# Weights of eight channel steps at staggered start addresses in an attention, gating and mixing kernel

## The chip, the core and the metric

The kernel runs on one core of one Trainium2 chip. The metric is the device time of a run in microseconds, the median of three runs. TensorE does the matmuls: it loads 128 columns of weights (the stationary operand) and then streams the moving operand past them, 512 columns at most. VectorE, ScalarE and GpSimd do the element-wise work, and SyncE, GpSimd and ScalarE issue DMAs. The on-chip memory SBUF has 128 partitions; a tile takes the same range of byte addresses in each of them, and all start addresses below are byte addresses within a partition.

## The reference

```python
scores = scale * q @ k^T - log(S)            # 4 batches, 12 heads, S = 448, head 64
x  = sigmoid(scores) @ v                     # -> x of 4 x 448 x 768
g  = sigmoid(causal_conv5(x, conv_w))
x  = (g * (x @ w_val)) @ w_out
u  = x + (relu(x^T @ w_tok1) @ w_tok2)^T     # token mixing
out = u + relu(u @ w_ch1) @ w_ch2            # channel mixing, 768 -> 1536 -> 768
```

The weights come as 64-bit floats, whose words the kernel decodes itself into a high and a low part of 32 bits. A product of two such split numbers takes three matmuls (high by high, low by high, high by low).

## The kernel before

The kernel runs through three stages. The first is attention, two heads at a time (lines 256 and 271). The second goes batch by batch through the value and output projections (line 334, 448 columns), the transposes (line 357) and the two token products (lines 374 and 387). The third is the channel stage, which is what the change touches.

The channel stage works on the 1792 rows of u in four column tiles of 512, 512, 384 and 384 (`TILES`). For each of them it goes through 12 channel steps of 128 hidden channels. `ch1(t, fc)` multiplies u by the step's part of `w_ch1` (18 matmuls: 6 row blocks of 768, three each; line 674); ScalarE and VectorE make the relu and its split into a high and a low tile `r` (lines 86 and 88). `ch2(t, fc)` multiplies `r` by the step's part of `w_ch2` into six accumulators (18 matmuls, line 695). The order is written by hand: ch1 of the next step stands ahead of ch2 of the step before, so that blocks of 18 matmuls of ch1 and ch2 alternate and the relu of one step lies beside a block of the other. Between two blocks nothing else runs on TensorE.

The weights of a step are four tiles side by side of 768 columns of 4 bytes: the high and the low part for ch1, and the same for ch2. They stay in SBUF for all four column tiles. Steps 1 to 3 lie in tiles `w` on the left side of SBUF, which the value projection used before; step 0 lies in a tile `wch0` on the left, and steps 4 to 11 each in a tile `wch4` to `wch11` of 12,288 bytes on the right side, where they are allocated one after the other from step 11 to step 4 (`wch_alloc`, at the start of the channel stage). In the kernel before, the right-hand tiles lie at 122,624 (wch11), 134,912 (wch10) and so on in steps of 12,288 up to 208,640 (wch4), all of them multiples of 256. So do all other tiles that TensorE reads in this stage: the moving operands (`us`, the split u, and `r`) and the tiles `w` and `wch0`. Two small tiles, `pad_l` of 160 bytes and `pad_r` of 224 bytes, stand at the outer ends of both sides.

The tile of step 4 is filled by four DMAs from a scratch area in HBM (`pre_load`, line 613, on GpSimd's queue), since its weights were decoded earlier. Steps 5 to 11 are decoded during the first column tile: two loads on SyncE's queue for each step (lines 578 and 583), and then for each a chain of operations that ends with a product on VectorE (line 132, the low part) and a copy on ScalarE (line 140, the high part) into the wch tile. They are given a low priority, so that the evictions of the matmuls go ahead of them.

Of the kernel before, what the change touches and what calls it, by code (L numbers as in the profile page):

```python
# [10 lines left out]
F32R = mybir.dt.float32r  # L11
# [19 lines left out]
def tile_kernel(ctx, tc, qT, kT, v, w_val, conv_w, w_out, w_tok1, w_tok2, w_ch1, w_ch2, out):  # L31
# [10 lines left out]
    DM = H * D  # L42
    P = 128
# [527 lines left out]
    wch, us_t, acc, r_t = {}, {}, {}, {}  # L571
    wch_t, r_b = {}, []
# [40 lines left out]
                nc.gpsimd.dma_start(wch[fc][which][a], wscr[PRE.index(fc), which, a])  # L613

    def wch_alloc(pool, fc):
        wch_t[fc] = pool.tile([P, 2, 2, DM], F32R, name=f"wch{fc}")

    def dec_ch(fc):
        for which in range(2):
# [85 lines left out]
    with tc.manual_schedule():  # L705
# [23 lines left out]
        for b in range(B):  # L729
            val, outs, t1, t2 = dense_steps(b)  # L730
            if b:

                weave(val[0] + back1 + sum(val[1:], []) + back2, first.pop(0), 0.95)
            else:
                val = sum(val, [])
                for n in (12, 8, 4):
                    val.insert(n, (0, dec_step))
                weave(val, [])
                assert not (begun or raws or decs)
                dec.release()  # L740
                dn["late"] = tc.alloc_tile_pool(name="late", bufs=1, side="right", reuse_waits="tile")
                pre = tc.alloc_tile_pool(name="pre", bufs=1, side="left")
                ops = ch_ops(pre, [(fc, which) for fc in PRE for which in range(2)])
                first = [ops[: len(ops) // 2], ops[len(ops) // 2 :]]
            if b + 1 < B:
                weave(outs, post_ops(b + 1))
            else:
                os = outs + t1 + t2
            back1, back2 = t1, t2
            if b + 2 == B:  # L750
                pre.release()
                xbp.release()
                rp["a"] = tc.alloc_tile_pool(name="p2a", bufs=1, side="left")
                wch_alloc(rp["a"], 0)
                first.append(ch_ops(rp["a"], [(0, 0), (0, 1)]))
# [15 lines left out]
    for fc in range(KF - 1, CHAN_HELD - 1, -1):  # L771
        wch_alloc(rp["p"], fc)
# [63 lines left out]
```

## Time and profile before

| | us |
|---|---|
| three runs | 731.84, 732.78, 732.80 |
| median | 732.78 |
| span of the profiled execution | 729.8 |
| TensorE matmuls busy | 724.2 (99%) |
| TensorE weight loads busy, beside the matmuls | 594.1 (81%) |
| VectorE busy | 398.9 (55%) |
| ScalarE busy | 256.7 (35%) |
| GpSimd busy | 40.2 (6%) |

The span runs from the first to the last instruction of one profiled execution. It has no timed run of its own; the difference to the median, 3.0 us, is what lies around it. The page calls TensorE's matmuls PE and its weight loads PEld. Matmuls are pipelined: one lasts 389 ns at 512 columns, but the next begins before it ends, so the pace is read from the starts of blocks and not from the length of one.

### The profile page before, as it was taken

How to read it: one execution, taken by the hardware profiler on the slowest of the kernel's cores; microseconds unless marked ns; L12 is line 12 of the kernel's file. 1: busy time of each engine (PE TensorE's matmuls, PEld its weight loads, DVE VectorE, ACT ScalarE, POOL GpSimd, SP SyncE). 2: the span in 40 equal slices, each digit the busy share in tenths (PEclk: the TensorE clock that was granted, in tenths of full speed). 3: DMA queues.
4: the chain of work that ended last, by engine and by line, in shares of the span. 5: the costliest groups of instructions: out<-in, count | busy, mean ns of one | idle time of the engine just before them, and what ended most of it. 6: DMA issues, size and time to landing. Idle time of an engine off the chain costs nothing.

```text
span 729.8 us, 10824 instructions
## 1 busy us (share of the span) xinstructions
PE 724.2 (99%) x4360; PEld 594.1 (81%) x4360; DVE 398.9 (55%) x690; ACT 256.7 (35%) x379; POOL 40.2 (6%) x90
## 2 busy tenths in 40 slices
PE   8999999999999999999999999999999999999998
PEld 3344444799999999999998888888888899999997
DVE  1899766489889878965577999320100400040002
ACT  6899888344334333422343434200000200020000
POOL 0001100000111111002012000000000000000000
PEclk9999999999999999999999999999999999999999
DMA  9847997221344232044927453250000610042001
GB/s 298 252 153 236 266 299 234 83 91 47 102 150 147 76 127 101 17 147 131 311 82 227 162 172 127 67 172 0 1 0 1 201 38 0 1 128 67 1 1 65
DMA packets 56737, 87.24 MB, mean 120 GB/s; under 512 B 8032, under 2 KB 48240, under 8 KB 56688
## 3 DMA queue, kind: packets, MB, share of 16 engines
q1 hardware_dynamic: 50352, 62.86, 28.1%
q0 software_dynamic: 5904, 23.23, 9.0%
q8 instruction: 34, 0.56, 0.3%
q10 hardware_dynamic: 432, 0.46, 0.2%
q14 instruction: 15, 0.12, 0.1%
HBM read 66.68 MB, written 19.86 MB: 119 GB/s over the span
## 4 chain that ended last, share of the span: by engine, by line
PE 98%; ACT 1%; DVE 1%; issue 0%; ACTq 0%
PE psd L334 24%; PE psh L674 24%; PE pso L695 24%; PE pss L256 8%; PE psy L271 8%; PE pst L374 4%; PE pst L387 4%; PE pst L357 1%; ACT ga L258 1%; PE psi L718 0%; DVE dec_a L123 0%; DVE w L132 0%; ACT dec_a L111 0%; DVE dec_e L129 0%; DVE ur L701 0%
## 5 line engine op out<-in xcount | busy, mean ns | idle before, releaser
L88 DVE SCALAR_TENSOR_TENSOR r<-psh,r 128x384 fp32r<-128x384 f32 (+1 forms) x47 | 29.3, 623 | 213.4 <-ACT r L86 213.4
L674 PE MATMUL psh<-us,wch 128*128 128x512 f32 (+1 forms) x648 | 135.5, 362 | 0.0
L695 PE MATMUL pso<-r,wch 128*128 128x384 f32 (+1 forms) x630 | 131.1, 361 | 0.0
L674 PEld LDWEIGHTS psh<-us,wch 128*128 128x128 f32 x648 | 117.3, 188 | 12.7
L695 PEld LDWEIGHTS pso<-r,wch 128*128 128x128 f32 x630 | 113.8, 188 | 11.9
L86 ACT ACTIVATE r<-psh 128x384 fp32r<-128x384 f32 (+1 forms) x47 | 25.5, 543 | 230.7 <-PE psh L674 230.6
L334 PE MATMUL psd<-gv,wo 128*128 128x448 f32 x432 | 92.3, 369 | 0.0
L258 ACT ACTIVATE ga<-pss,bias_s 128x896 f32<-128x896 f32 x84 | 83.6, 1005 | 19.0 <-PE pss L256 18.2
L334 PE MATMUL psd<-xs,w 128*128 128x448 f32 x432 | 89.9, 367 | 0.0
L334 PEld LDWEIGHTS psd<-xs,w 128*128 128x128 f32 x432 | 80.9, 188 | 8.2 <-issue 0.7
L334 PEld LDWEIGHTS psd<-gv,wo 128*128 128x128 f32 x432 | 80.2, 188 | 6.6
L256 PE MATMUL pss<-q,k 64*64 64x448 f32 x672 | 78.5, 537 | 1.0 <-ACT ga L258 0.9
L271 PE MATMUL psy<-ga,v 64*64 64x448 f32 x672 | 77.6, 536 | 0.0
L304 DVE SCALAR_TENSOR_TENSOR gate<-xb,cw,gate 128x448 f32<-128x448 f32 x96 | 65.7, 685 | 2.8
L256 PEld LDWEIGHTS pss<-q,k 64*64 64x64 f32 x672 | 26.0, 133 | 39.4 <-issue 29.0
L271 PEld LDWEIGHTS psy<-ga,v 64*64 64x64 f32 x672 | 25.7, 133 | 37.4 <-issue 35.9
L111 ACT ACTIVATE dec_a<-dec_a,exp_b 128x768 int32<-128x768 int32 (+3 forms) x43 | 36.8, 868 | 37.1 <-DVE dec_a L108 37.1
L123 DVE SCALAR_TENSOR_TENSOR dec_a<-raw,dec_a 128x768 int32<-128x768 int32 (+2 forms) x42 | 37.3, 888 | 19.7 <-ACT dec_a L111 19.7
L674 PE MATMUL psh<-us,w 128*128 128x512 f32 (+1 forms) x216 | 45.2, 362 | 0.0
L695 PE MATMUL pso<-r,w 128*128 128x512 f32 (+1 forms) x216 | 45.1, 362 | 0.0
L674 PEld LDWEIGHTS psh<-us,w 128*128 128x128 f32 x216 | 39.1, 188 | 4.3
L695 PEld LDWEIGHTS pso<-r,w 128*128 128x128 f32 x216 | 39.1, 188 | 4.2
(80 smaller groups left out, 648.7 us busy)
## 6 DMA issues: line engine op xcount, KB each, us to landing
raw<-w_ch SPq DMA_DIRECT2D x24, 768.0 KB, 4.4
v<-v SPq DMA_DIRECT2D x24, 224.0 KB, 6.5
uscr<-x2T POOLq DMA_DIRECT2D x24, 224.0 KB, 3.7
q<-qT SPq DMA_DIRECT2D x23, 224.0 KB, 4.3
k<-kT SPq DMA_DIRECT2D x22, 224.0 KB, 4.5
raw<-w_out POOLq DMA_DIRECT2D x6, 768.0 KB, 8.4
wscr<-pre POOLq DMA_DIRECT2D x12, 384.0 KB, 3.6
xscr<-xb SPq DMA_DIRECT2D x18, 224.0 KB, 4.7
```

What stands on the lines that cost most here:

```text
L88: nc.vector.scalar_tensor_tensor(out=l_out, in0=src, scalar=0.0, in1=f(h_out), op0=ALU.max, op1=ALU.subtract)
L111: nc.scalar.activation(out=t["a"], in_=t["a"], func=AF.Relu, scale=8.0, bias=exp_b)
L123: nc.vector.scalar_tensor_tensor(out=t["a"], in0=hi, scalar=-0x80000000, in1=t["a"], op0=ALU.bitwise_and, op1=ALU.bitwise_or)
L256: nc.tensor.matmul(ps[cols, j, :S], k[rows, keys], q[rows], start=True, stop=True)
L258: nc.scalar.activation(out=a, in_=ps[:, :, :S], func=AF.Sigmoid, bias=bias_s, scale=QK_SCALE)
L271: nc.tensor.matmul(y_t[i + h][cols, :S], v_t[i][rows, c, cols], a[rows, j], start=c == 0, stop=c == NB - 1)
L304: nc.vector.scalar_tensor_tensor(out=acc, in0=x[:, t : t + S], scalar=w, in1=acc, op0=ALU.mult, op1=ALU.add)
L334: nc.tensor.matmul(ps[:, :S], w(a, kk), s[:, c, :], start=kk == 0 and n == 0, stop=kk == KD - 1 and n == 2,)
L374: nc.tensor.matmul(ps[:, :HALF], a, x[:, m], start=n == 0, stop=n == len(mm) - 1)
L387: nc.tensor.matmul(ps[:, :S], a, m[:, t, :], start=t == 0 and n == 0, stop=t == KT - 1 and n == 2)
L674: nc.tensor.matmul(ps[:, :n_t], wch[fc][0][a][:, kk * P : (kk + 1) * P], us_t[t, kk][:, c, :], start=kk == 0 and n == 0, stop=kk == KD - 1 ...
L695: nc.tensor.matmul(acc[j][:, :n_t], wch[fc][1][a][:, j * P : (j + 1) * P], r[c], start=fc == 0 and n == 0, stop=fc == KF - 1 and n == 2,)
```

## The change

The tile of a step is allocated with 8 more elements of 4 bytes at its end, for all steps but step 0, and its first 4 x 768 columns are used as before. Since the eight tiles of steps 11 to 4 lie one after the other down from the same upper end, each begins 32 bytes further off a multiple of 256 than the next higher step: wch11 at 122,368 (0 modulo 256), wch10 at 134,688 (32), wch9 at 147,008 (64), wch8 at 159,328 (96), wch7 at 171,648 (128), wch6 at 183,968 (160), wch5 at 196,288 (192) and wch4 at 208,608 (224). No other tile moves. Each engine has the same instructions in the same order with the same waits as before.

```diff
     def wch_alloc(pool, fc):
-        wch_t[fc] = pool.tile([P, 2, 2, DM], F32R, name=f"wch{fc}")
+        t = pool.tile([P, 4 * DM + (8 if fc else 0)], F32R, name=f"wch{fc}")
+        wch_t[fc] = t[:, : 4 * DM].rearrange("p (n a m) -> p n a m", n=2, a=2)
```

## Rows read from the trace of the kernel before

**Rows 1.** The page: span; TensorE's busy time, share, instructions; its granted clock, 40 slices.
```profile
span 729.8 us, 10824 instructions
...
PE 724.2 (99%) x4360; PEld 594.1 (81%) x4360; DVE 398.9 (55%) x690; ACT 256.7 (35%) x379; POOL 40.2 (6%) x90
...
PEclk9999999999999999999999999999999999999999
```

**Rows 2.** The page: the chain that ended last, share of the span by line.
```profile
PE psd L334 24%; PE psh L674 24%; PE pso L695 24%; PE pss L256 8%; PE psy L271 8%; PE pst L374 4%; PE pst L387 4%; PE pst L357 1%; ACT ga L258 1%; PE psi L718 0%; DVE dec_a L123 0%; DVE w L132 0%; ACT dec_a L111 0%; DVE dec_e L129 0%; DVE ur L701 0%
```

**Rows 3.** Waits of TensorE in the whole run: us in total, times, longest.
```profile
PE psi L718 <- DVE zero L707: 1.2, 1, 1.2
PE pss L256 <- ACT ga L258: 0.9, 3, 0.4
```

**Rows 4.** Timeline of TensorE: start us, length us, line, output and inputs, columns, count.
```profile
409.04 4.24 PE L674 MATMUL psh<-us,wch 128*128 128x512 f32 x18
413.12 4.24 PE L695 MATMUL pso<-r,w 128*128 128x512 f32 x18
417.19 4.24 PE L674 MATMUL psh<-us,wch 128*128 128x512 f32 x18
...
466.15 4.01 PE L674 MATMUL psh<-us,wch 128*128 128x512 f32 x17
```

**Rows 5.** The chain in order of time: start us, us, what.
```profile
568.32 4.08 PE pso L695 x18
572.40 3.14 PE psh L674 x18
575.54 4.12 PE pso L695 x18
579.66 3.14 PE psh L674 x18
...
604.65 3.12 PE psh L674 x18
```

**Rows 6.** Matmuls in four short stretches from 575.4 us: busy us, mean ns of one.
```profile
L695 PE MATMUL pso<-r,wch 128*128 128x512 f32 x10 | 2.5, 393 | 0.0
...
L695 PE MATMUL pso<-r,wch 128*128 128x512 f32 x9 | 2.2, 389 | 0.0
...
L674 PE MATMUL psh<-us,w 128*128 128x384 f32 x7 | 1.4, 338 | 0.0
...
L674 PE MATMUL psh<-us,w 128*128 128x384 f32 x12 | 2.2, 334 | 0.0
```

**Rows 7.** Timeline of TensorE, projections of 448 columns, in two stretches.
```profile
132.73 22.15 PE L334 MATMUL psd<-xs,w 128*128 128x448 f32 x108
154.72 1.58 PE L334 MATMUL psd<-gv,wo 128*128 128x448 f32 x7
...
194.42 18.75 PE L334 MATMUL psd<-xs,w 128*128 128x448 f32 x90
213.01 0.57 PE L387 MATMUL pst<-wt2H,h 128*128 128x448 f32 x2
```

**Rows 8.** Weight loads by form: busy us, mean ns of one, idle before.
```profile
L674 PEld LDWEIGHTS psh<-us,wch 128*128 128x128 f32 x648 | 117.3, 188 | 12.7
...
L357 PEld LDWEIGHTS pst<-ident,x2T 128*128 128x128 f32 x96 | 11.9, 140 | 1.7
```

**Rows 9.** Two stretches: us, busy us and count of each engine, granted clock, DMA.
```profile
409.00:474.20 65.20, 65.20 (x289) 53.98 (x288) 51.38 (x74) 25.72 (x34) 0.00 (x0) 1.00 0.40 127
...
598.00:648.00 50.00, 50.00 (x291) 50.00 (x290) 7.49 (x14) 6.97 (x14) 0.00 (x0) 1.00 0.04 10
```

**Rows 10.** Timelines: VectorE's last product into a wch tile; GpSimd's four DMAs for wch4.
```profile
455.29 0.96 DVE L132 SCALAR_TENSOR_TENSOR wch<-raw,dec_e 128x768 fp32r<-128x768 f32 x1
...
386.18 2.18 POOL L613 DMA_DIRECT2D wch<-wscr  x4
```

**Rows 11.** DMA issues: KB each, median us from issue to landing.
```profile
wch<-wscr POOLq DMA_DIRECT2D x4, 384.0 KB, 6.5
```

## The prediction

> **What bounds the kernel now.** I read the page first: the span is 729.8 us, TensorE is busy for 99% of it, and its granted clock is at full in all 40 slices [rows 1]. The span is the profiled execution's own; the three timed runs have a median of 732.78 us, so about 3.0 us of a run lie outside the span, and I add these 3.0 us to every span below. The shares of the chain that ended last come next: nearly all of it is TensorE, and the two lines of the channel stage, 674 and 695, hold 24% each [rows 2]. The waits of TensorE add up to 2.1 us in the whole run, all of it near the start [rows 3]. So no transfer, no decode and no eviction is late anywhere in the channel stage, and what decides the time there is the pace at which one matmul follows another.
>
> The pace is read from the blocks of 18 matmuls that ch1 and ch2 issue in turn. A block on the weights w, a block on the weights wch and the next one start 4.07 to 4.08 us apart [rows 4], and the chain gives 4.08 us for a block of 512 columns and 3.12 us for one of 384 [rows 5]. That is 226.7 and 173.3 ns for a matmul. The 128 columns between them cost 53.3 ns, so 512 columns by themselves are 213.3 ns, and every matmul pays 13.3 ns on top, at either width.
>
> **What the change does, part by part.** The order of instructions and the waits are the same on every engine before and after; what differs is where eight tiles begin. wch11 stays at a multiple of 256 bytes, wch10 begins 32 bytes past one, wch9 64, and so on to wch4 at 224. All other operands of TensorE in this stage (us, r, w, wch0) keep starting at multiples of 256. Three things touch the moved tiles.
>
> First, what fills them: 14 products of the decode on VectorE and 14 copies on ScalarE write wch5 to wch11, and four DMAs fill wch4. The last VectorE product starts at 455.29 us and takes 0.96 us [rows 10]; the first block that reads wch11 starts at 466.15 us [rows 4], so there are 9.9 us of room. In the stretch from 409 to 474 us VectorE is busy for 51.4 of 65.2 us [rows 9]; even if each of the 14 products took twice its 0.96 us, the 13.4 us more would still fit in the 13.8 us that are free. The DMAs for wch4 are issued by 388.4 us [rows 10], land some 6.5 us later [rows 11], and the first block on wch4 starts at 409.04 us [rows 4]: 14 us of room. I cost all this at nothing, hidden by TensorE's own blocks; the cover would be gone only if a write became some ten microseconds late.
>
> Second, the size: each tile is 32 bytes longer, the eight together reach 256 bytes lower, and no wait was added by that. Nothing.
>
> Third, TensorE's weight loads, which is all that is left. Seven of the eight steps (4 to 10) have a new offset. A step has 36 matmuls on each of four column tiles, so 7 x 36 x 4 = 1008 weight loads and matmuls, 504 at 512 columns and 504 at 384, in 56 blocks of 18. The trace of before has no matmul of this kind with a weight that begins off a multiple of 256 bytes, so the cost has to be bounded by the nearest rows.
>
> That the pace isn't fixed by the instruction alone does stand in the trace. Where the width switches, the block takes longer for a while: the 512-column block that follows one of 384 columns took 4.12 us where the others take 4.08, and the two 384-column blocks beside it 3.14 where the others take 3.12 [rows 5]. Inside them it is the first matmuls: the first ten of the 512-column block last 393 ns each, the later nine 389; at 384 columns 338 for the first seven and 334 for the later ones [rows 6]. So a stream that is disturbed runs about 4 ns a matmul slower until it falls back into its regular beat. The 448-column projections show the same without any switch: 108 matmuls from 132.73 to 154.72 us are 203.6 ns each, 90 matmuls of the same form from 194.42 to 213.01 us are 206.6 ns each [rows 7], where halfway between the paces at 384 and 512 columns would be 200.0. The same form on the same tiles thus has more than one beat, 3.0 ns apart.
>
> The weights' offset changes at the border of blocks: into ch1 of step 4 (0 to 224), out of it into ch2 of step 3 (224 to 0), then at every border until the block after ch2 of step 10, 17 borders on each column tile, 68 in all, half at each width. **Low end of the forecast:** each such border disturbs the beat as a switch of width does, 34 x 0.04 + 34 x 0.02 = 2.0 us. **High end:** the 1008 matmuls never find a good beat. With the 4 ns of a disturbed stream that is 4.0 us; with the 6.6 ns by which the slow beat at 448 columns stands over 200.0 it is 6.6 us. I take the low end, 2.0 us, since a change of operand at the border of a block is nearest to the rows of the switch, where the beat was found again within the block; the other ends go into the range.
>
> Below nothing: no row shows a matmul of the channel stage at a lasting faster beat, but the 13.3 ns that each pays on top of its columns are there to be lost, 1008 x 13.3 = 13.4 us at the very most. The only gain of which a row gives the size is the 3.0 ns between the two beats at 448 columns, 1008 x 3.0 = 3.0 us.
>
> The sum: 729.8 + 2.0 = 731.8 us of span, and with the 3.0 us around it **734.8 us**.
>
> **The rivals.** *No difference.* The offset of the weights may not matter to TensorE at all. For it speaks that w, wch0 and wch stand at different multiples of 256 bytes and that ch1 takes its moving operand from us and ch2 from r, and yet their blocks are alike to 0.01 us [rows 4, 5]: none of these address bits shows. Against it speaks that these rows hold only multiples of 256, and that the beat reacts to small disturbances. The time is then that of before, 732.8 us. The Trainium skill has a rule for this (TensorE: Matmul & The Clock Gate, Step-by-step: what each phase is for): TensorE reads the moving operand and the weights through two independent ports of SBUF, so that loading the next weights takes nothing from the running matmul. By that rule nothing of the change can reach the pace, and the time stays. The trace bears it out only in part: load and matmul do overlap, but the 13.3 ns on top and the two beats at 448 columns are not explained by columns alone.
>
> *Faster.* If the 13.3 ns come from weight and moving reads that meet because both begin at multiples of 256, a spread of starts would thin them out. With the 3.0 ns above this is 729.8 us in a run. It decides if most of the seven offsets have a better beat than 0. Against it: the disturbances in rows 5 and 6 all go up, and the regular beat is the best that these blocks show.
>
> *The weight load becomes the bound.* At 384 columns the weight loads leave no gap, 50.00 of 50.00 us [rows 9], and one takes 188 ns [rows 8] where a matmul follows each 173.3 ns. How long a load is does vary between forms: the one of the transposes, 128 columns of 4 bytes as well, takes 140 ns [rows 8]. If a start off 256 bytes made a load touch three stretches of 256 bytes instead of two, I bound what that could add by this difference of 48 ns: 504 x 48 = 24.2 us at 384 columns; at 512 columns 226.7 - 188 = 38.7 ns hide the first part and 504 x 9.3 = 4.7 us remain. Together 28.9 us, 761.7 us. It decides from the point where a load is visibly longer than 188 ns. Against it: the length of a load did not react in any block, at either width.
>
> **How the numbers follow.** The forecast, a disturbed or slower beat between 734.8 and 739.4 us, gets 0.44; the load as the bound 0.05; no difference 0.35; faster 0.16. A measurement of this kernel can tell 0.2%, 1.5 us, from no change. So slower 0.49, same 0.35, faster 0.16. The range takes in no change, most of the gain of 3.0 us and the forecast to its high end (732.8 + 6.6): 730.0 to 739.4 us. Left out are the load as the bound, gains beyond it and the rest of the tail, some 0.15. Slower and no difference both weigh much; the forecast's own range is 734.8 to 739.4.
>
> **What would show it.** Right: in the chain the blocks on wch4 to wch10 read 4.10 to 4.20 us at 512 columns and 3.14 to 3.24 at 384, loads stay at 188 ns, blocks on w and on wch11 fall back to 4.08 and 3.12, TensorE's waits stay near 2 us, and everything before 409 us stays as it is. No difference: all blocks stay at 4.08 and 3.12. Faster: some blocks below 4.08 or 3.12, by offset. The load as the bound: loads longer than 188 ns, and 384-column blocks hit much harder than those of 512. My reasoning would be wrong altogether if a wait on a filled wch tile appeared on TensorE, or if stages without a moved tile changed their pace.

## The result, and the profile after

The changed kernel takes 736.93 us in the median of three runs (736.79 to 737.64), before 732.78. The ratio is 1.0062 with a 95% interval of 1.0046 to 1.0077: slower by 4.15 us, 0.6%. It lies in the stated range and on the forecast side, at about twice the forecast price of 2.0 us.

On the page of after TensorE is still busy all the time, and its weight loads are as long as before. First the page (span, busy time), then groups by form (busy us, mean ns of one, idle before):

```profile
span 734.9 us, 10824 instructions
...
PE 729.4 (99%) x4360; PEld 595.4 (81%) x4360; DVE 398.7 (54%) x690; ACT 256.6 (35%) x379; POOL 40.1 (5%) x90
...
PEclk9999999999999999999999999999999999999999
```

```profile
L675 PE MATMUL psh<-us,wch 128*128 128x512 f32 x324 | 78.0, 394 | 0.0
L696 PE MATMUL pso<-r,wch 128*128 128x512 f32 x306 | 73.7, 394 | 0.0
L675 PE MATMUL psh<-us,wch 128*128 128x384 f32 x324 | 59.6, 337 | 0.0
...
L675 PE MATMUL psh<-us,w 128*128 128x512 f32 x108 | 25.5, 389 | 0.0
...
L675 PEld LDWEIGHTS psh<-us,wch 128*128 128x128 f32 x648 | 117.6, 188 | 14.3
```

The matmuls on wch lengthened from 389 to 394 ns at 512 columns and, in ch1, from 334 to 337 at 384; those of ch1 on w stayed at 389, and a load is 188 ns as in [rows 8]. The waits of TensorE sum to 2.0 us, none of them on a filled wch tile. The chain shows the blocks one by one (start us, us, what); the first seven are at 512 columns, the rest at 384:

```profile
406.10 4.09 PE pso L696 x18
410.18 4.20 PE psh L675 x18
414.39 4.11 PE pso L696 x18
418.50 4.13 PE psh L675 x18
...
443.56 4.22 PE psh L675 x18
...
460.37 4.19 PE psh L675 x18
...
468.75 4.12 PE psh L675 x18
...
599.49 3.12 PE pso L696 x18
602.62 3.19 PE psh L675 x18
...
608.92 3.12 PE psh L675 x18
...
615.23 3.18 PE psh L675 x18
...
627.87 3.12 PE psh L675 x18
```

The reader is to see that the blocks differ by offset, and not in the same way at both widths. The block at 410.18 is ch1 on wch4 (offset 224), at 418.50 on wch5 (192), at 443.56 on wch8 (96), at 460.37 on wch10 (32); the one at 468.75 is on wch11, which begins at 0, and the one at 414.39 on w, also at 0. At 384 columns the blocks stand for offsets 224 (602.62), 192 (608.92), 160 (615.23) and 96 (627.87). Before, the blocks took 4.08 or 3.12 us, but for those at a switch of width [rows 5]. Of those shown here at 512 columns, the blocks at offset 0 take 4.09 to 4.12 us, the one at 192 takes 4.13, and the others 4.19 to 4.22. At 384 columns two of the four moved blocks, at 224 and 160, take 3.18 or 3.19 us, and the two at 192 and 96 stay at 3.12.

Worked out from the starts of all matmuls of ch1 and ch2 (72 for each offset other than 0 and each width, 360 for offset 0), the distance from one matmul to the next exceeds the 226.7 or 173.3 ns of before by:

| offset of the weights | 512 columns, ns | 384 columns, ns |
|---|---|---|
| 0 | 0.7 (before: 0.3) | 0.4 (before: 0.1) |
| 32 | 6.2 | 0.2 |
| 64 | 6.6 | 0.7 |
| 96 | 7.3 | 0.0 |
| 128 | 6.4 | 2.9 |
| 160 | 6.4 | 3.1 |
| 192 | 3.0 | 0.2 |
| 224 | 6.7 | 3.4 |

Times their counts these are 3.06 us for the 504 moved matmuls at 512 columns and 0.76 us for the 504 at 384. The matmuls at offset 0 cost 0.42 us, of which before has 0.16 itself, at the start of the stage and at the switch of width; so 0.26 us are new, in blocks that lie beside moved ones. Together the channel stage takes 4.08 us more, against 4.15 us between the medians. The spans differ by more, 5.1 us. The rest is at the start of the program: the first projection starts at 133.6 us instead of 132.7. There the first 16 matmuls of the scores took 2.96 us in this execution and 1.90 us in that of before; why is left open. The same 16 took 1.91 us in e2, 2.53 in e3 and 2.84 in e1 below, so this varies from execution to execution and none of it belongs to the change.

### The profile page after: what moved, and what is told of

Its sections match the earlier page's. It is cut to its first block, busy times and chain, and to the rows that moved or that the text cites. A ratio compares the mean times of both kernels' runs of the same rounds, so it can differ in the third digit from the quotient of the medians.

```text
span 734.9 us, 10824 instructions
## 1 busy us (share of the span) xinstructions
PE 729.4 (99%) x4360; PEld 595.4 (81%) x4360; DVE 398.7 (54%) x690; ACT 256.6 (35%) x379; POOL 40.1 (5%) x90
## 4 chain that ended last, share of the span: by engine, by line
PE 97%; DMA 1%; ACT 1%; DVE 0%; issue 0%; SPq 0%; ACTq 0%
PE psd L334 24%; PE psh L675 24%; PE pso L696 24%; PE psy L271 8%; PE pss L256 8%; PE pst L374 4%; PE pst L387 4%; PE pst L357 1%; DMA k<-kT 1%; ACT ga L258 0%; DVE dec_a L123 0%; DVE w L132 0%; ACT dec_a L111 0%; DVE dec_e L129 0%; DVE ur L702 0%
## 5 line engine op out<-in xcount | busy, mean ns | idle before, releaser
L675 PE MATMUL psh<-us,wch 128*128 128x512 f32 (+1 forms) x648 | 137.6, 365 | 0.0
L696 PE MATMUL pso<-r,wch 128*128 128x384 f32 (+1 forms) x630 | 133.0, 364 | 0.0
```

The lines of the kernel that those rows point to most:

```text
L675: nc.tensor.matmul(ps[:, :n_t], wch[fc][0][a][:, kk * P : (kk + 1) * P], us_t[t, kk][:, c, :], start=kk == 0 and n == 0, stop=kk == KD - 1 ...
L696: nc.tensor.matmul(acc[j][:, :n_t], wch[fc][1][a][:, j * P : (j + 1) * P], r[c], start=fc == 0 and n == 0, stop=fc == KF - 1 and n == 2,)
```

## Experiments

Three theories stood after this. **Difference**: the beat follows from weight start minus moving start, modulo 256 bytes. **Start**: the weight's own start counts. **Border**: only a change of offset from one block to the next costs. All kernels below start from the kernel before; a shift is that of the start address, modulo 256. The paces at 448 columns are distances of starts worked out from the trace, as in the table.

**Left side shifted: e1_left96.**

```diff
-    const.tile([P, 40], F32, name="pad_l")
+    const.tile([P, 64], F32, name="pad_l")
```

> The kernel before with everything on the left side of SBUF 96 bytes higher: u (the moving operand of ch1), w and wch0 begin 96 bytes off a multiple of 256; r (the moving operand of ch2) and wch4 to wch11 stay at 0. Difference theory (the pace follows from weight start minus moving start, modulo 256; values from the profile of after): ch1 on wch4 to wch11 has the difference 160, 4.20 us a block at 512 columns and 3.18 at 384; ch2 on w and wch0 has 96, 4.20 and 3.12; ch1 on w and wch0 and ch2 on wch4 to wch11 have 0 and stay at 4.08 and 3.12 apart from some first matmuls. 288 x 6.5 + 288 x 3.0 + 144 x 7.2 ns = 3.8 us, with borders 3.8 to 5 us more than before. Start theory (the weight's own start counts): both ch1 and ch2 on w and wch0 are slow, 288 x 7.2 ns = 2.1 us, and all blocks on wch4 to wch11 stay at 4.08 and 3.12. Border theory (only a change of offset between blocks costs): 4.12 and 3.14 in the first block after each change, blocks settle within ten matmuls.

Measured: 737.49 us against 732.36 us for before on the same chip, ratio 1.0067 (1.0050 to 1.0084). The chain:

```profile
401.87 4.11 PE psh L674 x18
405.97 4.20 PE pso L695 x18
410.18 4.20 PE psh L674 x18
414.37 4.20 PE pso L695 x18
418.57 4.20 PE psh L674 x18
422.77 4.12 PE pso L695 x18
426.89 4.21 PE psh L674 x18
...
593.51 3.18 PE pso L695 x18
596.69 3.12 PE psh L674 x18
```

At 512 columns, the block at 401.87 is ch1 on w: both operands are at 96, the difference is 0, and it takes 4.11. The ch2 blocks at 405.97 and 414.37 read w at 96 against r at 0 and take 4.20; the ch1 blocks at 410.18, 418.57 and 426.89 read wch, which did not move, against the moved u and take 4.20 to 4.21; ch2 on wch4 (422.77) has difference 0 again and takes 4.12. The start theory has ch1 on w slow and ch1 on wch at 4.08: it falls. The border theory falls as well: the blocks on wch stay at 4.20 to 4.21 to their end and do not settle. The difference theory holds in every block at 512 columns, and the 5.1 us measured lie just above its 3.8 to 5 us. One miss: at 384 columns all eight ch2 blocks on w and wch0 (difference 96) took 3.18 us, as the one at 593.51, where the table has 3.12 for the same difference. Weights at 96 and moving operand at 0 are the starts of the 384-column ch2 blocks on wch8 in after, too. So at this width the two starts modulo 256 do not fix the pace alone.

**Everything shifted: e2_all32.**

```diff
-    const.tile([P, 40], F32, name="pad_l")
+    const.tile([P, 48], F32, name="pad_l")
-    pad_r.tile([P, 56], F32, name="pad_r")
+    pad_r.tile([P, 48], F32, name="pad_r")
```

> The kernel before with both sides of SBUF 32 bytes higher, so that every operand of TensorE, moving and weights, begins 32 bytes off a multiple of 256. Difference theory: all differences are 0 as before, every block stays at 4.08 and 3.12 us, the time within 0.2% of before. Start theory: weights at 32 cost 6.2 ns a matmul at 512 columns and 0.2 at 384, 864 x 6.2 + 864 x 0.2 ns = 5.5 us more than before at least, with every 512-column block at 4.19 us. Border theory: no change of offset anywhere, the time of before.

Measured: 733.40 against 732.36 us, ratio 1.0018 (1.0008 to 1.0027). The channel stage is that of before in every block:

```profile
410.65 4.08 PE psh L674 x18
414.73 4.08 PE pso L695 x18
418.81 4.08 PE psh L674 x18
...
615.46 3.12 PE pso L695 x18
618.58 3.12 PE psh L674 x18
```

Weights at 32 cost 6.2 ns a matmul in after and nothing here, where the moving operands stand at 32 too. So nothing is special about multiples of 256, and the start theory falls here too. The 1.0 us is outside the channel stage: the out projection went from 206.5 to 208.2 ns on average, 0.7 us. It follows transposes, whose moving identity did not move; that the two belong together is an inference.

**One offset for all eight: e3_uniform96.**

```diff
+    rp["p"].tile([P, 40], F32, name="pad_w")
     r_b += [rp["p"].tile([P, 2, W], F32R, tag="r", bufs=2, name="r") for _ in range(2)]
```

> The kernel before with wch4 to wch11 all 96 bytes off a multiple of 256, everything else at 0: the same 56 blocks and more are off, but only 6 borders on a column tile change the offset instead of 17. Difference theory and start theory: every 512-column block on wch4 to wch11 takes 4.20 us, every 384-column block 3.12; 576 x 7.2 ns = 4.1 us more than before. Border theory: 24 borders instead of 68, 0.7 us by the switch rows and 1.5 us by scaling the 4.15 us measured; blocks in the middle of a run of wch settle at 4.08.

Measured: 737.54 against 732.36 us, ratio 1.0070 (1.0055 to 1.0085), 5.2 us with 24 borders where after had 68. In the channel stage of the profiled execution, the fastest of the four, it is 4.5 us by the starts of its matmuls, where after has 4.1.

```profile
409.85 4.21 PE psh L674 x18
414.06 4.08 PE pso L695 x18
418.14 4.22 PE psh L674 x18
422.36 4.21 PE pso L695 x18
426.57 4.22 PE psh L674 x18
...
464.53 4.22 PE pso L695 x18
...
615.93 3.12 PE psh L674 x18
```

Between 418 and 477 us no block changes its offset, and each takes 4.21 to 4.22, to the last: nothing settles at 4.08. So a change of offset is not what costs. The 384-column blocks stay at 3.12, as the difference theory has it for 96, but for a few of 3.13 to 3.15 beside a change of offset. One offset for all costs no less than a spread: 96 is the dearest of them at 512 columns, and eight steps are moved here instead of seven.

**The same in the 448-column stage: s1 to s4, e4.** Here each kernel shifts the moving operand of the value projection (xs) within its tile, and the right side below the weights by a pad, so that the gated tiles (moving operand of the out projection), the transposed tiles and h1 move; e4 shifts xs alone, by 16 bytes. The channel stage stays as in before. The diff is that of s1; the others put 16, 40, 56 and 4 in place of 8, and 32, 48, 56 and none in place of 16.

```diff
-        xs = both.tile([P, 2, W], F32R, tag="xs", bufs=KD, name="xs")[:, :, :S]
+        xs = both.tile([P, 2, W], F32R, tag="xs", bufs=KD, name="xs")[:, :, 8 : 8 + S]
+    wts.tile([P, 16], F32, name="pad_g")
     wt1H = wts.tile([P, NF + 1, NTOK], F32R, name="wt1H")
```

Expected of s1:

> The channel stage is as in before. In the 448-column stage the moving operand of the value projection begins 32 bytes off (difference 224), and the gated tiles, the transposed tiles and h1 begin 64 bytes lower (out projection and first token product: difference 64; second token product: 192). Difference theory: the channel stage stays at 4.08 and 3.12; the projections leave their two beats of 202.7 and 206.7 ns and each takes a beat of its own, between 200 and 214 ns by the spread of 13 ns seen in after (0 to +7 over the beat at difference 0); first token product near 174.0 ns. Start theory: the value projection stays as before, since w did not move; the out projection stays as before, since wo did not move; the second token product, whose weights h1 moved, changes. No dependence at 448 columns: the time of before.

Expected of s2:

> As s1, other offsets: value projection at difference 192, out projection at 128, first token product at 128, second at 128; channel stage as before. Difference theory: a beat of its own for each; the second token product of s1 at 192 ran at 200.0 ns in the stretches without transposes, so the value projection should run at 200 to 202 instead of 205.5 on average, 432 x 4 ns = 1.7 us less; the out projection at 128 unknown, 200 to 207 ns. Chance theory (at 448 columns the beat depends on what came before, not on the difference): value projection near 205.5 as before.

Expected of s3:

> As s1, other offsets: value projection at difference 96, out projection and first token product at 192, second token product at 64; channel stage as before. Difference theory: out projection at 200 to 202 ns in the stretches without transposes, against 206.5 on average before; second token product near the 202.3 of the out projection of s1 at 64; first token product at 173.4. Chance theory: averages as before, 205.5 and 206.5.

Expected of s4:

> As s1, other offsets: value projection at difference 32, out projection and first token product at 224, second token product at 32; channel stage as before. Difference theory: first token product slower, near the 176.7 ns of after at 224; out projection with the beats of the value projection of s1 at 224 (200.0, 204.3 and 206.7, mean 206); value projection unknown, 200 to 207. Chance theory: averages as before.

Expected of e4:

> The kernel before with the moving operand of the value projection 16 bytes off a multiple of 256, difference 240, all else at 0. If the difference counts in steps of 32 bytes or more, the value projection keeps the beats of difference 0 (202.7 and 206.7 ns, mean 205.5); if in finer steps, beats that were not seen before. The out projection stays at 206.5 and the channel stage at 4.08 and 3.12 us.

Measured, with the difference (weights minus moving) and the mean pace of the 432 matmuls of each projection:

| kernel | value projection | out projection | time, us | ratio to before (95%) |
|---|---|---|---|---|
| before | 0: 205.5 ns | 0: 206.5 ns | 732.4 to 732.6 | |
| s1 | 224: 206.1 | 64: 204.7 | 731.19 | 0.9983 (0.9974 to 0.9992) |
| s2 | 192: 200.6 | 128: 206.1 | 730.30 | 0.9970 (0.9959 to 0.9981) |
| s3 | 96: 200.8 | 192: 202.7 | 728.65 | 0.9947 (0.9932 to 0.9962) |
| s4 | 32: 204.5 | 224: 207.5 | 732.14 | 0.9994 (0.9985 to 1.0003) |
| e4 | 240: 202.6 | 0: 206.7 | 730.99 | 0.9978 (0.9969 to 0.9987) |

The difference 192 gives its beat in whichever projection has it, the out projection being slower by the matmuls that restart after each set of transposes (about 290 ns each). The pace away from those is 200.0 ns. At difference 0 the value projection has 205.5 to 205.9 ns in before, after, e1, e2 and e3, so chance does not explain the 200.6 and 200.8 ns of s2 and s3: the theory that at 448 columns chance decides falls. Neither start sets the pace alone: for the value projection of s2 and s3 only the moving operand moved, and for the second token product of s1 only the weights did, which ran at 199.8 ns in its first form, restarts left out, against 205.0 in before. When both move together, by 96 in e1 or by 32 in e2, the value projection keeps 205.9 and 205.7 ns.

Not all came out as expected. In s1 the value projection at difference 224 can't be told from difference 0 by its average. In e4 a shift of only 16 bytes gives a pattern seen in no other run (206, 203, 198 ns in turn), so the effect is finer than 32 bytes. For s4 only the averages come near what was expected of the out projection (205.2 ns without the restarts, 206 expected); its value projection was left open, and its first token product came out at 175.0 instead of 176.7 ns.

**Put to use: c1, c2, c3.** c1 is s1 with 16 in place of 8 and 48 in place of 16: both projections at 192.

> Both projections at difference 192, first token product at 192, second at 64; channel stage as before. Difference theory: both projections at 200 to 202 ns, 432 x 4 + 432 x 4.5 ns = 3.7 us less than before, about 0.5%, the first kernel clearly faster than before. Chance theory: the time of before.

Measured: 728.24 against 732.41 us, ratio 0.9952 (0.9937 to 0.9968), 4.2 us faster than before and not to be told from s3; one of its ten runs took 733.8 us and is not explained, the others 728.0 to 728.6. First the timeline of c1 (start us, length us), the 90 projections of [rows 7], then groups by form of c1 and, below them, of before (busy us, mean ns of one):

```profile
194.46 18.16 PE L335 MATMUL psd<-xs,w 128*128 128x448 f32 x90
212.46 0.57 PE L388 MATMUL pst<-wt2H,h 128*128 128x448 f32 x2
```

```profile
L335 PE MATMUL psd<-gv,wo 128*128 128x448 f32 x432 | 90.7, 365 | 0.0
L335 PE MATMUL psd<-xs,w 128*128 128x448 f32 x432 | 87.8, 362 | 0.1
...
L334 PE MATMUL psd<-gv,wo 128*128 128x448 f32 x432 | 92.3, 369 | 0.0
L334 PE MATMUL psd<-xs,w 128*128 128x448 f32 x432 | 89.9, 367 | 0.0
```

The 90 now take 212.46 - 194.46 = 18.00 us, 200.0 ns each, where before took 206.6. By the distances of starts the two projections together gain 432 x 5.0 + 432 x 3.8 = 3.8 us of the 4.2.

Two variants try other choices for the out projection and the token products. c2 puts 40 and 24 into the diff of s1; c3 puts 40 and 16, and a pad of 32 elements behind the weights of the second token product.

Expected of c2:

> Both projections and the first token product at difference 96, second token product at 160; channel stage as before. Difference theory: value projection at 200.8 ns as in s3 (432 x 4.7 ns = 2.0 us less), out projection near 202 including the matmuls after transposes (432 x 4.5 = 1.9 us less), first token product at 173.4 to 176.6; about 728.5 us. Chance theory: out projection at its 206.5 of before, 730.4 us.

Expected of c3:

> Value projection at difference 96, out projection at 192, first token product at 64, second at 192; channel stage as before. Difference theory: value projection 200.8, out projection 202.7 ns, second token product as in s1 (209.0 and 202.0 by line 387's two forms instead of 211 to 213 and 205 to 207; 0.5 us less than c1), first token product as in s1 (174.7; 0.2 us more than c1): near 728 us. Chance theory: single averages come out elsewhere than in the runs from which they are taken.

Measured: c2 730.17 us, ratio 0.9964 (0.9952 to 0.9976); c3 729.07 us, ratio 0.9954 (0.9941 to 0.9967). c3 is no better than c1. Its projections came out as expected (200.6 and 202.8 ns), and so did the second token product: one of its forms averages 207.3 ns, but that is one pause of 467 ns, in which the weight load of the next value projection waits for a copy on ScalarE; the other 47 matmuls average 201.8. c1 has the same pause. The first token product was slower than expected, 175.7 ns against 174.7. c2 is a miss and shows a limit: at the same difference 96 the value projection ran at 200 ns in 418 of 432 matmuls, but of the out projection only about half did, the other half at 206.7, 205.6 on average. Groups by form of c2:

```profile
L335 PE MATMUL psd<-gv,wo 128*128 128x448 f32 x432 | 91.9, 367 | 0.0
L335 PE MATMUL psd<-xs,w 128*128 128x448 f32 x432 | 87.8, 363 | 0.0
```

So a difference can carry more than one beat, and no run here tells what decides between them. What runs ahead of a stretch is one possibility. Another that was not tested is that address bits above 256 count where the difference is not 0: the high and the low half of xs lie 2,048 bytes apart, those of the gated tiles 1,792.

## Why the prediction was right, point by point

**The bound.** Right: no wait on the filling of a tile appeared, order and loads stayed, and 4.08 of the 4.15 us are in the pace of the channel stage's matmuls.

**The covers.** Writes and DMAs into the moved tiles cost nothing, as costed: TensorE waits 2.0 us in all, as before.

**The sign.** Right, and for the reason given against *Faster*: the regular beat of the channel stage was the best that its blocks have, at 512 columns clearly (0 is below all seven others), at 384 with several offsets as good.

**The size.** This is the step that failed, though inside its bounds: "I take the low end, 2.0 us, since a change of operand at the border of a block is nearest to the rows of the switch, where the beat was found again within the block". The beat is not found again. A moved block runs in a short pattern of its own from its first matmul to its last, and e3 shows it with hardly a border. The other end, that the 1008 matmuls never find the good beat, is nearest to what happened; with 4 ns for each it gave 4.0 us and the measurement 4.15. That agreement is luck: 4 ns was taken for both widths, and it is 6.1 ns at 512 columns (3.06 us / 504) and 1.5 at 384 (0.76 / 504), where only the offsets 128, 160 and 224 cost more than 0.7 ns. The sign named for 384 columns, blocks of 3.14 to 3.24 us, therefore held for three offsets of the seven. A border price is there too, but it is the small part, 0.26 us in the blocks at offset 0.

**The sum.** The 3.0 us added to the span are not what lies around a span. The profiled executions of the later kernels, whose times are known, lie 1.9 us above their spans (736.79 for 734.9 in after); by that the execution profiled of before took about 731.7 us, an estimate, and was one of the shorter ones. The median came out right because the 3.0 us were made to give it.

**The rivals.** *No difference* rested on blocks that are alike at multiples of 256, and on the rule of the Trainium skill (TensorE: Matmul & The Clock Gate, Step-by-step: what each phase is for) that loading the next weights takes no read bandwidth from the running matmul. The first is true and says nothing on smaller offsets. Against the second, the traces show that where the weights lie changes the pace of the matmuls beside which they are loaded, by up to 7.3 ns of 226.7; the measurement decides. *Faster* was right that the starts of weights and moving operand count together (that their reads meet is not shown), but not for this stage: at 448 columns difference 0 is a poor choice, and 192 wins, and 96 in the value projection. *The load as the bound* did not happen: 188 ns throughout.

## What to carry to other kernels

This rests on one kernel, with weights of 128 x 128 elements of 4 bytes. Where TensorE never waits and loads new weights for each matmul, compare the distance of successive starts with what the columns alone would take; if the same form shows two paces, look at weight start minus moving start modulo 256 bytes, and sweep it per stage with the spare room that a tile already has. A good difference for one width is not one for another (0 was best at 512 columns, 192 at 448), so choose the two starts relative to each other and not by a round address, and price an offset by a lasting pace of each width, not by a passing disturbance.

## What the runs showed of the hardware

The pace of these matmuls depends on the difference of two start addresses modulo 256 bytes, in steps of 16 bytes at the finest tried, and not on either address alone (e1, e2). The mechanism behind it is not shown. The best lasting paces are 173.3, 200.0 and 226.7 ns at 384, 448 and 512 columns, evenly spaced, so that 13.3 ns beyond the 53.3 ns for each 128 columns stay at every width; no offset tried held a faster pace. A difference may hold two beats (3.12 and 3.18 us a block at 384 columns with 96; 200.0 and 206.7 ns at 448 with 96). The page's busy share does not show any of this: TensorE reads 99% in before, in after and in c1.
